# Retention and a two-layer ffn on one core: coefficients pinned behind retention, weights laid out by tiles, three raw buffers

## Chip, cores and metric

The kernel runs on one core of a Trainium2 chip. The time is device microseconds of one execution. Lower is better.

## What is computed

```python
def _attn_ref(q, k, v):                      # (4, 8, 576, 64) each
    scores = (1.0 / np.sqrt(D_)) * np.matmul(q, k.transpose(0, 1, 3, 2))
    gamma = 1.0 - 2.0 ** (-5.0 - np.arange(H, dtype=np.float32))
    Dmat = np.where(rel >= 0, gamma[:, None, None] ** rel[None, :, :], 0.0)
    return np.matmul(scores * Dmat[None, :, :, :], v)

def _moe_ref(x, w_in, w_out, a, b):          # x (2304, 512), w_in (512, 2048)
    h = x @ w_in
    P = a[0] + a[1] * h + a[2] * h**2 + a[3] * h**3
    Q = 1.0 + np.abs(b[0]) * np.abs(h) + np.abs(b[1]) * h**2
    return (P / (Q + 1e-06)) @ w_out

def _moe2_ref(x, w_in, w_out, s, b):
    r = np.maximum(x @ w_in, 0.0)
    return (s * (r * r) + b) @ w_out

# reference: x = _attn_ref(...) laid out (2304, 512); _moe_ref; then _moe2_ref
```

The weights `w_in` and `w_out` of both layers come as float64, everything else as float32. A float64 is read as two 32-bit words.

## The kernel before

**Retention** (`retention`, L147 to L293) runs over 16 pairs of heads. For each pair SP loads three tiles (`loads`, L173): `xT` (queries and keys, 576 KB), `vn` (values, 320 KB), `kn` (keys, 256 KB). They come from pools of `IN_BUFS` = 6 buffers; the load for a later pair waits until PE, and for `vn` POOL too, has done with the buffer. The loop over pairs (L276) issues, for pair p: the loads of pair p + 5; `value_state` (L237, PE: queries times the state left by earlier chunks); `state(p + 1)` (L225, PE, then ACT L228 and DVE L229); one step of cutting a weight; `scale(p + 3)` (L196, POOL multiplies values by a decay); `value_chunk` (L245, PE: masked scores times values; then DVE L248 makes `x`, ACT L250 its high part `xh`, POOL L251 its low part `xl`); `scores(p + 1)` (L214, PE; then DVE L217 multiplies by the mask into `pm`).

**Weights.** The ffn takes 32 weights kf: 16 column blocks in each of the two layers. One weight is 128 columns of `w_in` and the 128 rows of `w_out` that belong to them, 512 KB each. `w_load` (L100) brings both into a `raw` buffer with two DMAs on SP (L104, L106); there are `RAW_BUFS` = 2 such buffers. `w_cut` (L108) turns the words into a float32 number and splits it into a high and a low part, in five steps:

```python
pin(nc.scalar.activation(m, f, AF.Abs))                          # L120 ACT
pin(nc.vector.tensor_scalar(lo, lo, ...))                        # L121 DVE, end of step 1
pin(nc.vector.tensor_scalar(m, m, ...)); rest(...)               # L123, L124 DVE, step 2
rest(nc.vector.scalar_tensor_tensor(out=t, in0=hi, ...))         # L126 DVE, step 3
rest(nc.vector.scalar_tensor_tensor(out=hi..., in0=lo, ...))     # L129 DVE, step 4
rest(nc.scalar.copy(whf, f))                                     # L136 ACT, step 5
nc.gpsimd.tensor_tensor(out=wlf, in0=f, in1=f32(whf), ...)       # L137 POOL
next_load()                                                      # the next weight into a free raw buffer
```

The first three weights (`W_FIRST`) are cut within retention, one step in each turn of the pair loop from p = 1; the load of weight 2 is issued behind the low part of weight 0. The next weights are cut in the ffn.

**ffn** (L296). Blocks of 512 or 256 tokens times one weight make a unit u: 12 matmuls into `h` (L326 to L328), an activation on ACT, POOL and DVE (first layer L346 to L377, second L382 to L387), then 12 matmuls into `o` (L411), which DVE adds to `acc` (L423). `aneg` = -a (L513, DVE) and `babs` = |b| (L512, ACT) are its coefficients, from `a_sb` and `b_sb`, which `small_loads` (L253) loads.

**What sets the order.** Each engine, and SP's queue of loads, works through its own instructions strictly in order. The order comes from a scheduler that works with estimated times and may move an instruction forward if what it needs is there. `tc.keep_in_program_order` (`pin`, `dve`, `pe`) binds an instruction behind the one that was traced just before it on its engine, and only behind that one. Most of retention is pinned; `aneg`, `babs` and the small loads are not, nor are the cuts from weight 5 on (the first steps of weights 3 and 4 are).

Of the kernel before, what the change touches and what calls it, by code (L numbers as in the profile page):

```python
# [11 lines left out]
I32 = mybir.dt.int32  # L12
U32 = mybir.dt.uint32
I64 = mybir.dt.int64
AF = mybir.ActivationFunctionType
ALU = mybir.AluOpType
# [12 lines left out]
W_BUFS = 5  # L29
W_EARLY = 4  # L30
WTMP_BUFS = 1
RAW_BUFS = 2
IN_BUFS = 6
G_BUFS = 3
T_BUFS = {"ta": 2, "tq": 2, "tt": 4}
H_BUFS = 4
# [3 lines left out]


@with_exitstack
def retention_ffn_kernel(ctx, tc, w_in1, w_out1, a, b, w_in2, w_out2, s2, b2, qkv, maskv, gdec, out):
    nc = tc.nc
    B, H, S, D = SHAPE
    NT, DM = out.shape
    DFF = w_in1.shape[1]
    P = 128
    NP = H // 2
    NC = DM // P  # L50
    NF = DFF // P
    NCH = (S + P - 1) // P
    TAIL = S - (NCH - 1) * P
    NMAIN = S // P
# [23 lines left out]
        return t.bitcast(F32)  # L78


    w_src = [(w_in1, w_out1), (w_in2, w_out2)]
    w_raw = {}
    w_t = {}
    w_slots = {}
# [13 lines left out]
    w_slot_tiles(wpool, range(W_EARLY))  # L98

    def w_load(kf, eng, pin):  # L100
        layer, f = divmod(kf, NF)
        wi, wo = w_src[layer]
        w_raw[kf] = t = stg.tile([P, 2, DM], I64, tag="raw", name=f"raw{kf}")
        pin(eng.dma_start(out=t[:, 0, :].rearrange("p (c f) -> p c f", c=NC),  # L104
                          in_=wi[:, f * P:(f + 1) * P].rearrange("(c p) f -> p c f", p=P)))
        pin(eng.dma_start(out=t[:, 1, :], in_=wo[f * P:(f + 1) * P, :]))  # L106

    def w_cut(kf, pinned=False):  # L108

# [8 lines left out]
        pin(nc.scalar.activation(m, f, AF.Abs))  # L120
        pin(nc.vector.tensor_scalar(lo, lo, 2.0 ** 28, 2.0 ** 32 - 256, op0=ALU.add, op1=ALU.min))  # L121
        yield
        pin(nc.vector.tensor_scalar(m, m, 2.0 ** -15, None, op0=ALU.max))  # L123
        rest(nc.vector.tensor_scalar(t, t, 5, 2, op0=ALU.logical_shift_left, op1=ALU.logical_shift_right))  # L124
        yield
        rest(nc.vector.scalar_tensor_tensor(out=t, in0=hi, scalar=-0x40000000, in1=t,  # L126
                                            op0=ALU.bitwise_and, op1=ALU.bitwise_or))
        yield
        rest(nc.vector.scalar_tensor_tensor(out=hi.bitcast(U32), in0=lo, scalar=29, in1=t.bitcast(U32),  # L129
                                            op0=ALU.logical_shift_right, op1=ALU.bitwise_or))  # L130
        yield
        wh, wl = w_slots[kf % W_BUFS]
# [14 lines left out]
    def retention(actx):  # L147
# [25 lines left out]
        def loads(p, other=lambda: None):  # L173

            if p >= NPAIR:
                return
            n1, n2, n3 = 2 * S, 2 * S + NCH * P, 2 * S + NCH * P + NM
            xT[p] = sbr.tile([P, 2, S], F32, tag="xT", name=f"xT{p}")
            vn[p] = sbr.tile([P, NCH, 2, D], F32, tag="vn", name=f"vn{p}")
            kn[p] = sbr.tile([P, NMAIN, 2, D], F32, tag="kn", name=f"kn{p}")  # L180
            pin(nc.sync.dma_start(out=xT[p].rearrange("p x t -> p (x t)"), in_=qkv[p, :, 0:n1]))
            other()
            pin(nc.sync.dma_start(out=vn[p].rearrange("p c h d -> p (c h d)"), in_=qkv[p, :, n1:n2]))
            pin(nc.sync.dma_start(out=kn[p].rearrange("p c h d -> p (c h d)"), in_=qkv[p, :, n2:n3]))
# [75 lines left out]
        pin(nc.sync.dma_start(out=odec[:, :, 0:P], in_=gdec.rearrange("p (h t) -> p h t", t=P)))  # L260
        for p in range(1, IN_BUFS):
            loads(p)
            if p in (3, IN_BUFS - 1):
                next_load(nc.sync, pin)

        steps = (s for kf in range(W_FIRST) for s in w_cut(kf, True))
# [9 lines left out]
        for p in range(NPAIR):  # L276
            if p:
                loads(p - 1 + IN_BUFS)
            if p == 8:
                small_loads()  # L280
            value_state(p)
            if 0 < p < NPAIR - 1:
                state(p + 1)
            if p > 0:
                next(steps, None)
            scale(p + 3)
            value_chunk(p)
            if p + 1 < NPAIR:
                scores(p + 1)
            if p == 0:  # L290
                state(p + 1)
# [217 lines left out]
    nc.scalar.preload_act_table_set("natural_log_exp_and_others")  # L509
    with ExitStack() as actx:  # L510
        retention(actx)
    nc.scalar.activation(babs, b_sb, AF.Abs)  # L512
    nc.vector.tensor_scalar(aneg, a_sb, -1.0, None, op0=ALU.mult)  # L513
    with ExitStack() as fctx:
        ffn(fctx)


_INS = ["moe_w_in", "moe_w_out", "moe_a", "moe_b", "moe2_w_in", "moe2_w_out", "moe2_s", "moe2_b"]
_OUT = ((2304, 512), "float32")


# [56 lines left out]
```

## Time and profile before

| | us |
|---|---|
| runs (median of 3, lowest to highest) | 909.52 (907.26 to 909.61) |
| profiled execution | 911.61 |
| its span, first to last instruction | 909.8 |
| PE busy in the span | 872.0 (96%) |
| DVE, ACT, POOL busy | 603.4, 526.8, 358.4 |
| granted clock of TensorE, mean | 0.992 |

The span is the profiled execution's from its first to its last instruction; its own time also holds what lies around that. A share of busy time says little by itself: retention fills the first 95 us, the first layer runs to about 545 us, the second to the end, and each has another limit. The rows further below take them apart.

### The profile page before, as it was taken

To read this page: it belongs to the slowest core of one execution; us is meant where nothing else is said; L and a number is where in the kernel's file an instruction comes from. 1 tells how busy PE (TensorE), PEld (TensorE's weight loads), DVE (VectorE), ACT (ScalarE), POOL (GpSimd) and SP (SyncE) were. 2 spreads that over 40 slices of the span, in tenths; PEclk is the share of its full clock that TensorE was granted. 3 is DMA by queue.
4 is the path that set the end of the run, shared out by engine and by line. 5 is a ranking of instruction groups with operands and counts; after the bars stand their busy time and mean duration, and the time that the engine had idled before them with its cause. 6 is when DMAs were issued, how large, how long until landed. Compare 5 with 4: busy or idle time off the path is not lost.

```text
span 909.8 us, 12650 instructions
## 1 busy us (share of the span) xinstructions
PE 872.0 (96%) x4896; PEld 733.0 (81%) x4896; DVE 603.4 (66%) x905; ACT 526.8 (58%) x876; POOL 358.4 (39%) x248
## 2 busy tenths in 40 slices
PE   6798999999999999999999899999999999999997
PEld 6687787888788878878887678888888888888886
DVE  4587699697987887888998971435643465432334
ACT  2132688897877876777887574444444444443332
POOL 3486566576555565546688830111111111101000
PEclk9799999999999999999999999999999999999999
DMA  9972111111011111111101120111111012000013
GB/s 349 327 271 99 48 46 48 47 47 47 10 38 47 46 47 47 47 46 47 47 1 47 61 78 1 47 47 47 47 46 47 4 44 93 1 0 1 4 67 139
DMA packets 32317, 58.54 MB, mean 64 GB/s; under 512 B 2689, under 2 KB 19585, under 8 KB 32257
## 3 DMA queue, kind: packets, MB, share of 16 engines
q1 hardware_dynamic: 32256, 57.74, 18.2%
q8 instruction: 38, 0.62, 0.3%
q14 instruction: 23, 0.18, 0.1%
HBM read 53.01 MB, written 4.72 MB: 63 GB/s over the span
## 4 chain that ended last, share of the span: by engine, by line
PE 49%; DVE 21%; POOL 10%; DMA 9%; ACT 5%; issue 5%; SPq 1%; DVEq 0%; POOLq 0%; ACTq 0%
PE o L411 23%; PE h L328 8%; PE h L326 8%; PE h L327 8%; DMA raw<-in_moe_w_out_dram 6%; POOL wl L137 3%; DVE acc L423 2%; DVE tt L365 2%; POOL tq L348 2%; DVE h L366 2%; POOL gl L377 2%; DVE wm L126 2%; DVE tt L354 2%; DMA xT<-in_qkv_dram 2%; DVE raw L129 2%
## 5 line engine op out<-in xcount | busy, mean ns | idle before, releaser
L326 PE MATMUL h<-xl,wh 128*128 128x512 f32 (+1 forms) x640 | 236.6, 370 | 2.9 <-DVE tt L367 2.8
L327 PE MATMUL h<-xh,wl 128*128 128x512 f32 (+1 forms) x640 | 235.6, 368 | 0.0
L328 PE MATMUL h<-xh,wh 128*128 128x512 f32 (+1 forms) x640 | 235.5, 368 | 0.0
L137 POOL TENSOR_TENSOR wl<-raw,wh 128x1024 fp32r<-128x1024 f32 x32 | 80.0, 2501 | 278.2 <-ACT wh L136 278.2
L384 DVE TENSOR_SCALAR tt<-ta,s_sb,b_sb 128x512 f32<-128x512 f32 (+1 forms) x80 | 48.8, 610 | 143.1 <-ACT ta L383 142.9
L348 POOL TENSOR_TENSOR tq<-tq,ta 128x512 f32<-128x512 f32 (+1 forms) x80 | 104.1, 1301 | 100.2 <-ACT tq L347 98.3
L326 PEld LDWEIGHTS h<-xl,wh 128*128 128x128 f32 x640 | 120.5, 188 | 26.9 <-DVE tt L367 6.4
L328 PEld LDWEIGHTS h<-xh,wh 128*128 128x128 f32 x640 | 120.6, 188 | 20.4
L327 PEld LDWEIGHTS h<-xh,wl 128*128 128x128 f32 x640 | 120.6, 188 | 20.3
L411 PE MATMUL o<-gl,wh 128*128 128x512 f32 (+1 forms) x320 | 119.0, 374 | 8.8 <-POOL gl L377 6.2
L377 POOL TENSOR_TENSOR gl<-tt,gh 128x512 fp32r<-128x512 f32 (+1 forms) x80 | 105.0, 1314 | 34.0 <-ACT gh L372 31.7
L411 PE MATMUL o<-gh,wl 128*128 128x512 f32 (+1 forms) x320 | 117.9, 369 | 0.0
L411 PE MATMUL o<-gh,wh 128*128 128x512 f32 (+1 forms) x320 | 116.8, 368 | 0.0
L411 PE MATMUL o<-wh,gl 128*128 128x512 f32 x288 | 112.3, 390 | 0.4 <-DVE gl L387 0.4
L411 PE MATMUL o<-wh,gh 128*128 128x512 f32 x288 | 112.1, 389 | 0.0
L382 ACT ACTIVATE ta<-h 128x512 f32<-128x512 f32 (+1 forms) x80 | 44.3, 554 | 115.5 <-PE h L328 115.4
L411 PE MATMUL o<-wl,gh 128*128 128x512 f32 x288 | 94.0, 390 | 1.7 <-DVE acc L423 1.7
L386 ACT CAST gh<-tt 128x512 fp32r<-128x512 f32 (+1 forms) x80 | 46.2, 578 | 59.0 <-DVE tt L384 57.0
L387 DVE TENSOR_TENSOR gl<-tt,gh 128x512 fp32r<-128x512 f32 (+1 forms) x80 | 53.1, 664 | 39.4 <-ACT gh L386 39.4
L411 PEld LDWEIGHTS o<-gl,wh 128*128 128x128 f32 x320 | 60.2, 188 | 23.6 <-POOL gl L377 9.2
L423 DVE TENSOR_TENSOR acc<-acc,o 128x512 f32<-128x512 f32 (+1 forms) x114 | 69.5, 649 | 3.4 <-PE o L411 3.4
L359 ACT ACTIVATE ta<-tq,lnb 128x512 f32<-128x512 f32 (+1 forms) x80 | 54.6, 682 | 23.9 <-POOL tq L348 23.5
(51 smaller groups left out, 1414.7 us busy)
## 6 DMA issues: line engine op xcount, KB each, us to landing
raw<-in_moe_w_in_dram SPq DMA_DIRECT2D x32, 512.0 KB, 4.0
raw<-in_moe_w_out_dram SPq DMA_DIRECT2D x32, 512.0 KB, 4.9
xT<-in_qkv_dram SPq DMA_DIRECT2D x16, 576.0 KB, 7.2
vn<-in_qkv_dram SPq DMA_DIRECT2D x16, 320.0 KB, 6.6
out_dram<-acc SPq DMA_DIRECT2D x18, 256.0 KB, 2.2
kn<-in_qkv_dram SPq DMA_DIRECT2D x16, 256.0 KB, 6.9
mv<-in_maskv_dram SPq DMA_DIRECT2D x1, 310.0 KB, 4.2
odec<-in_gdec_dram SPq DMA_DIRECT2D x1, 256.0 KB, 5.7
```

Of the source, the lines that this page charges most:

```text
L137: nc.gpsimd.tensor_tensor(out=wlf, in0=f, in1=f32(whf), op=ALU.subtract)
L326: nc.tensor.matmul(ps, lhsT=wh[:, c, :], rhs=xl[:, c, r], start=c == 0, stop=False)
L327: nc.tensor.matmul(ps, lhsT=wl[:, c, :], rhs=xh[:, c, r], start=False, stop=False)
L328: nc.tensor.matmul(ps, lhsT=wh[:, c, :], rhs=xh[:, c, r], start=False, stop=c == NC - 1)
L348: nc.gpsimd.tensor_tensor(out=tq, in0=tq, in1=ta, op=ALU.mult)
L359: nc.scalar.activation(ta, tq, AF.Ln, bias=lnb, scale=QS)
L377: nc.gpsimd.tensor_tensor(out=gl, in0=tt, in1=f32(gh), op=ALU.subtract)
L384: nc.vector.tensor_scalar(tt, ta, s2_sb, b2_sb, op0=ALU.mult, op1=ALU.add)
L386: nc.scalar.copy(gh, tt)
L387: nc.vector.tensor_tensor(out=gl, in0=tt, in1=f32(gh), op=ALU.subtract)
L411: nc.tensor.matmul(ps, lhsT=lh, rhs=rh, start=st and x == 0, stop=sp and x == 2)
L423: nc.vector.tensor_tensor(out=at, in0=at, in1=ps, op=ALU.add)
```

## The change

1. `aneg` and `babs` are pinned behind what was traced before them: the last pair of retention.
2. The host lays the weights out by tiles: one array `w`, in which weight kf is 128 rows of 8 KB, `w_in` and `w_out` side by side. `w_load` issues one DMA of 1 MB in place of two.
3. `RAW_BUFS` goes from 2 to 3, `IN_BUFS` from 6 to 5. Weight 0 is loaded behind pair 2's inputs, weight 1 behind pair 4's, weight 2 in turn 2 behind pair 6's. The loop over pairs loads pair p + 4.
4. The steps of the first three cuts start in turn 3 and end in turn 14, which has two of them.

```diff
 W_BUFS = 5
 W_EARLY = 4
 WTMP_BUFS = 1
-RAW_BUFS = 2
-IN_BUFS = 6
+RAW_BUFS = 3
+IN_BUFS = 5
...
     def w_load(kf, eng, pin):
-        layer, f = divmod(kf, NF)
-        wi, wo = w_src[layer]
-        w_raw[kf] = t = stg.tile([P, 2, DM], I64, tag="raw", name=f"raw{kf}")
-        pin(eng.dma_start(out=t[:, 0, :].rearrange("p (c f) -> p c f", c=NC),
-                          in_=wi[:, f * P:(f + 1) * P].rearrange("(c p) f -> p c f", p=P)))
-        pin(eng.dma_start(out=t[:, 1, :], in_=wo[f * P:(f + 1) * P, :]))
+        w_raw[kf] = t = stg.tile([P, 2 * DM], I64, tag="raw", name=f"raw{kf}")
+        pin(eng.dma_start(out=t, in_=w[kf]))
...
         for p in range(1, IN_BUFS):
             loads(p)
-            if p in (3, IN_BUFS - 1):
+            if p in (2, 4):
                 next_load(nc.sync, pin)
...
             if p:
                 loads(p - 1 + IN_BUFS)
+            if p == 2:
+                next_load(nc.sync, pin)
...
-            if p > 0:
+            for _ in range((p > 2) + (p > 13)):
                 next(steps, None)
...
-    nc.scalar.activation(babs, b_sb, AF.Abs)
-    nc.vector.tensor_scalar(aneg, a_sb, -1.0, None, op0=ALU.mult)
+    tc.keep_in_program_order(nc.scalar.activation(babs, b_sb, AF.Abs))
+    tc.keep_in_program_order(nc.vector.tensor_scalar(aneg, a_sb, -1.0, None, op0=ALU.mult))
...
+def _by_tiles(w_in, w_out, P=128):
+    dm, dff = w_in.shape
+    wi = w_in.reshape(dm // P, P, dff // P, P).transpose(2, 1, 0, 3).reshape(dff // P, P, dm)
+    return np.ascontiguousarray(np.concatenate([wi, w_out.reshape(dff // P, P, dm)], axis=2)).view(np.int64)
```

How the order moves. The numbers behind the names are buffers and differ between the two kernels; a line of the changed kernel is lower by 4 to 6 (L121 is now L115, L513 now L509).

DVE of the kernel before, in turns 1 and 2: `x` of pair 1, then `aneg`, then the masked scores `pm` of pair 2 and the cut step 2 of weight 0.

```order
L229 TENSOR_TENSOR spre_108<-pv_252,spre_108 128x128
L121 TENSOR_SCALAR raw_136<-raw_136 128x1024
L248 TENSOR_TENSOR x_277<-pv_227,odec 128x576
L513 TENSOR_SCALAR aneg<-a_sb 128x4
L217 TENSOR_TENSOR pm_0_293<-sc_0_281,mv 128x576
L217 TENSOR_TENSOR pm_1_295<-sc_1_282,mv 128x576
L229 TENSOR_TENSOR spre_109<-pv_311,spre_109 128x128
```

`aneg` stands here in front of the masked scores of pair 2; in the changed kernel these come straight after `x` of pair 1, and the cut of weight 0 begins two turns later.

DVE of the changed kernel, from the last turns into the ffn (`raw_292` is weight 2, `raw_602` weight 3, `tt` the ffn's).

```order
L123 SCALAR_TENSOR_TENSOR raw_292<-raw_292,wm_843 128x1024
L242 TENSOR_TENSOR x_1013<-pv_937,odec 128x576
L211 TENSOR_TENSOR pm_0_1029<-sc_0_1017,mv 128x576
L211 TENSOR_TENSOR pm_1_1031<-sc_1_1018,mv 128x576
L242 TENSOR_TENSOR x_1051<-pv_987,odec 128x576
L509 TENSOR_SCALAR aneg<-a_sb 128x4
L115 TENSOR_SCALAR raw_602<-raw_602 128x1024
L350 TENSOR_TENSOR tt_1101<-tt_1101,h_1086 128x512
L351 SCALAR_TENSOR_TENSOR tt_1101<-tt_1101,aneg,h_1086 128x512
L350 TENSOR_TENSOR tt_1134<-tt_1134,h_1119 128x512
```

`aneg` and the first step of weight 3 (L115, in the kernel before it stood ahead of pair 11's `pm`) now stand between the last pair's `x` and the first operation of the ffn.

SP of the kernel before, behind pair 5's keys: weight 1, then the small loads around the inputs of pair 6.

```order
L181 DMA xT_145<-in_qkv_dram 128x1152
L183 DMA vn_146<-in_qkv_dram 128x640
L184 DMA kn_147<-in_qkv_dram 128x512
L104 DMA raw_151<-in_moe_w_in_dram 128x4x128
L106 DMA raw_151<-in_moe_w_out_dram 128x512
L254 DMA a_sb<-in_moe_a_dram 128x4
L181 DMA xT_238<-in_qkv_dram 128x1152
L255 DMA b_sb<-in_moe_b_dram 128x2
L256 DMA s_sb<-in_moe_s_dram 128x1
L257 DMA b_sb<-in_moe_b_dram 128x1
```

The first of the small loads is the one that `aneg` waits for; weight 1 stands behind pair 5's inputs.

SP of the changed kernel, from pair 4's values on (`raw_144` is weight 1).

```order
L177 DMA vn_139<-in_qkv_dram 128x640
L178 DMA kn_140<-in_qkv_dram 128x512
L100 DMA raw_144<-in_w_dram 128x1024
L248 DMA a_sb<-in_moe_a_dram 128x4
L249 DMA b_sb<-in_moe_b_dram 128x2
L250 DMA s_sb<-in_moe_s_dram 128x1
L251 DMA b_sb<-in_moe_b_dram 128x1
L175 DMA xT_230<-in_qkv_dram 128x1152
L177 DMA vn_231<-in_qkv_dram 128x640
L178 DMA kn_232<-in_qkv_dram 128x512
L175 DMA xT_286<-in_qkv_dram 128x1152
L177 DMA vn_287<-in_qkv_dram 128x640
```

Weight 1 and the four small loads now stand ahead of pair 5's inputs; weight 2 (`raw_292`) follows two rows further on, behind pair 6's.

DVE of the changed kernel in the ffn, where units 14 to 16 are worked on (`raw_1001` and `wm_1707` are weight 5, `wm_1941` weight 6).

```order
L363 SCALAR_TENSOR_TENSOR tt_1691<-h_1676,tt_1691 128x256
L115 TENSOR_SCALAR raw_1001<-raw_1001 128x1024
L350 TENSOR_TENSOR tt_1737<-tt_1737,h_1722 128x256
L351 SCALAR_TENSOR_TENSOR tt_1737<-tt_1737,aneg,h_1722 128x256
L361 SCALAR_TENSOR_TENSOR tt_1737<-tt_1737,aneg,h_1722 128x256
L362 SCALAR_TENSOR_TENSOR h_1722<-tq_1736,h_1722 128x256
L363 SCALAR_TENSOR_TENSOR tt_1737<-h_1722,tt_1737 128x256
L117 TENSOR_SCALAR wm_1707<-wm_1707 128x1024
L118 TENSOR_SCALAR wm_1707<-wm_1707 128x1024
L120 SCALAR_TENSOR_TENSOR wm_1707<-raw_1001,wm_1707 128x1024
L123 SCALAR_TENSOR_TENSOR raw_1001<-raw_1001,wm_1707 128x1024
L350 TENSOR_TENSOR tt_1782<-tt_1782,h_1767 128x512
```

Weight 5's steps stand here in one piece and weight 6's follow two rows later; before, they were spread over units 5 to 10. From about unit 25 on, DVE's cut operations stand at the same places as before, each for a weight one further on.

## Rows read from the trace of the kernel before

**Rows 1.** By stage: us; PE, PEld, DVE, ACT, POOL busy (instructions); clock; DMA share; GB/s
```profile
0.00:96.00 96.00, 76.73 (x1155) 70.92 (x1156) 59.98 (x87) 23.15 (x40) 52.81 (x38) 0.93 0.72 259
96.00:545.00 449.00, 435.27 (x2077) 361.11 (x2077) 386.37 (x576) 355.42 (x592) 278.82 (x199) 1.00 0.13 43
545.00:910.00 365.00, 359.96 (x1666) 300.92 (x1664) 157.07 (x243) 148.23 (x245) 26.74 (x11) 1.00 0.12 39
```

**Rows 2.** PE in time order: start, us, operation [idle before <-releaser]; turns 2, 3
```profile
21.77 0.99 PE L237 MATMUL pv<-xT,spre 64*64 64x128 f32 x16
30.33 2.85 PE L245 MATMUL pv<-pm,vn 128*64 128x128 f32 x20 [6.76 <-DVE pm L217]
35.44 1.43 PE L237 MATMUL pv<-xT,spre 64*64 64x128 f32 x16
```

**Rows 3.** DVE in time order, the work that PE waited for in turn 2
```profile
29.45 0.17 DVE L513 TENSOR_SCALAR aneg<-a_sb 128x4 f32<-128x4 f32 x1 [7.61 <-DMA a_sb<-in_moe_a_dram]
```

**Rows 4.** PE in time order, turns 11 and 12; then DVE within turn 11
```profile
70.86 0.99 PE L237 MATMUL pv<-xT,spre 64*64 64x128 f32 x16
75.89 0.43 PE L245 MATMUL pv<-pm,vn 128*64 128x128 f32 x2 [2.46 <-DVE pm L217]
80.27 1.21 PE L237 MATMUL pv<-xT,spre 64*64 64x128 f32 x16
...
73.55 1.62 DVE L121 TENSOR_SCALAR raw<-raw 128x1024 uint32<-128x1024 uint32 x1 [1.11 <-DMA raw<-in_moe_w_out_dram]
```

**Rows 5.** PE in time order, the last two turns and the first ffn matmul
```profile
88.56 0.99 PE L237 MATMUL pv<-xT,spre 64*64 64x128 f32 x16
92.55 0.99 PE L237 MATMUL pv<-xT,spre 64*64 64x128 f32 x16
95.26 0.50 PE L326 MATMUL h<-xl,wh 128*128 128x512 f32 x1
```

**Rows 6.** By stretch, columns as in rows 1: the clock and the DMA rate
```profile
10.00:15.00 5.00, 5.00 (x48) 4.76 (x50) 3.95 (x5) 0.39 (x1) 2.70 (x2) 1.00 1.03 406
30.00:35.00 5.00, 4.67 (x38) 4.18 (x40) 3.28 (x6) 1.03 (x3) 0.17 (x1) 0.50 0.94 312
35.00:40.00 5.00, 5.00 (x80) 4.68 (x80) 3.33 (x5) 0.27 (x1) 2.45 (x2) 0.86 0.95 335
```

**Rows 7.** DVE's two longest cut steps of weight 1; PE's turns 7 to 10
```profile
51.54 1.77 DVE L124 TENSOR_SCALAR wm<-wm 128x1024 int32<-128x1024 int32 x1
60.17 2.25 DVE L129 SCALAR_TENSOR_TENSOR raw<-raw,wm 128x1024 uint32<-128x1024 uint32 x1
...
51.93 0.99 PE L237 MATMUL pv<-xT,spre 64*64 64x128 f32 x16
57.76 0.99 PE L237 MATMUL pv<-xT,spre 64*64 64x128 f32 x16
61.75 0.99 PE L237 MATMUL pv<-xT,spre 64*64 64x128 f32 x16
66.87 0.99 PE L237 MATMUL pv<-xT,spre 64*64 64x128 f32 x16
```

**Rows 8.** POOL in time order, pair 5's values; SP's first load behind a cut
```profile
25.65 1.26 POOL L196 TENSOR_TENSOR vn<-vn,mv 128x640 f32<-128x640 f32 x1 [0.32 <-DMA vn<-in_qkv_dram]
...
49.76 0.38 SPq L104 DMA_DIRECT2D raw<-in_moe_w_in_dram  x1
```

**Rows 9.** ACT, then DVE, where the ffn begins
```profile
98.44 0.60 ACT L346 ACTIVATE ta<-h 128x512 f32<-128x512 f32 x1 [1.54 <-POOL xl L251]
...
99.80 0.69 DVE L354 TENSOR_TENSOR tt<-tt,h 128x512 f32<-128x512 f32 x1 [3.60 <-ACT tt L349]
```

**Rows 10.** Waits, whole program: total us, times, longest us
```profile
DVE raw L121 <- DMA raw<-in_moe_w_out_dram: 41.3, 22, 4.3
```

**Rows 11.** SP, then DVE: one load of the ffn and the step behind it
```profile
221.85 0.38 SPq L104 DMA_DIRECT2D raw<-in_moe_w_in_dram  x1
...
227.27 0.85 DVE L121 TENSOR_SCALAR raw<-raw 128x1024 uint32<-128x1024 uint32 x1 [4.22 <-DMA raw<-in_moe_w_out_dram]
```

More of the change, by code (lines that the diff above doesn't have):

```diff
@@ L42, in retention_ffn_kernel @@
 @with_exitstack
-def retention_ffn_kernel(ctx, tc, w_in1, w_out1, a, b, w_in2, w_out2, s2, b2, qkv, maskv, gdec, out):
+def retention_ffn_kernel(ctx, tc, a, b, s2, b2, w, qkv, maskv, gdec, out):
     nc = tc.nc
@@ L46, in retention_ffn_kernel @@
     NT, DM = out.shape
-    DFF = w_in1.shape[1]
     P = 128
@@ L50, in retention_ffn_kernel @@
     NC = DM // P
-    NF = DFF // P
+    NF = w.shape[0] // 2
     NCH = (S + P - 1) // P
@@ L78, in f32 @@
         return t.bitcast(F32)
-    w_src = [(w_in1, w_out1), (w_in2, w_out2)]
     w_raw = {}
@@ L100, in w_load @@
     def w_load(kf, eng, pin):
-        layer, f = divmod(kf, NF)
-        wi, wo = w_src[layer]
-        w_raw[kf] = t = stg.tile([P, 2, DM], I64, tag="raw", name=f"raw{kf}")
-        pin(eng.dma_start(out=t[:, 0, :].rearrange("p (c f) -> p c f", c=NC),
-                          in_=wi[:, f * P:(f + 1) * P].rearrange("(c p) f -> p c f", p=P)))
-        pin(eng.dma_start(out=t[:, 1, :], in_=wo[f * P:(f + 1) * P, :]))
+        w_raw[kf] = t = stg.tile([P, 2 * DM], I64, tag="raw", name=f"raw{kf}")
+        pin(eng.dma_start(out=t, in_=w[kf]))
     def w_cut(kf, pinned=False):
-        words = w_raw.pop(kf).rearrange("p w n -> p (w n)").bitcast(I32).rearrange("p (n two) -> p n two", two=2)
+        words = w_raw.pop(kf).bitcast(I32).rearrange("p (n two) -> p n two", two=2)
         lo, hi = words[:, :, 0].bitcast(U32), words[:, :, 1]
@@ L511, in retention_ffn_kernel @@
         retention(actx)
-    nc.scalar.activation(babs, b_sb, AF.Abs)
-    nc.vector.tensor_scalar(aneg, a_sb, -1.0, None, op0=ALU.mult)
+    tc.keep_in_program_order(nc.scalar.activation(babs, b_sb, AF.Abs))
+    tc.keep_in_program_order(nc.vector.tensor_scalar(aneg, a_sb, -1.0, None, op0=ALU.mult))
     with ExitStack() as fctx:
         ffn(fctx)
-_INS = ["moe_w_in", "moe_w_out", "moe_a", "moe_b", "moe2_w_in", "moe2_w_out", "moe2_s", "moe2_b"]
+_INS = ["moe_a", "moe_b", "moe2_s", "moe2_b"]
 _OUT = ((2304, 512), "float32")
@@ L564 @@
     given = {n: np.ascontiguousarray(inputs[n]) for n in _INS}
-    for n, arr in given.items():
-        if arr.dtype == np.float64:
-            given[n] = arr.view(np.int64)
+    given["w"] = np.concatenate([_by_tiles(np.asarray(inputs[n + "_w_in"]), np.asarray(inputs[n + "_w_out"]))
+                                 for n in ("moe", "moe2")])
     given["qkv"] = _by_pairs(*(np.asarray(inputs[n]) for n in "qkv"))
```

## The prediction

> **What bounds the kernel now.** I read the busy time by stage first. From 96 us on PE is the limit: it is busy for 435.27 of 449 us while the first layer runs and for 359.96 of 365 us in the second, at a granted clock of 1.00 [rows 1]. Before 96 us, in retention, it is not: 76.73 of 96 us at a clock of 0.93 [rows 1]. So a gain has to come mostly from retention, and I count there in turns of the pair loop. Turn k starts with the first matmul of L237 for pair k.
>
> A turn without trouble lasts 92.55 - 88.56 = 3.99 us, and the last one, which has no next pair, 95.26 - 92.55 = 2.71 us [rows 5]. Turn 2 starts at 21.77 [rows 2]. Thirteen such turns and the last would bring the first ffn matmul to 21.77 + 13 x 3.99 + 2.71 = 76.35 us. It starts at 95.26, so turns 2 to 15 hold 18.91 us of delay. Two turns have most of it. Turn 2 lasts 35.44 - 21.77 = 13.67 us: PE stands still for 6.76 us before the value matmuls [rows 2], because DVE stood for 7.61 us before `aneg`, an operation of 0.17 us that waits for the DMA of `a_sb` [rows 3]. The masked scores that PE needs are queued behind it. PE's clock is then at 0.50, its lower level of 1.2 GHz, from 30 to 35 us [rows 6], so the turn pays for the stall twice: 13.67 - 3.99 = 9.68 us. Turn 11 lasts 80.27 - 70.86 = 9.41 us: DVE's first cut step of weight 3 waits 1.11 us for its DMA and takes 1.62 us, and PE stands for 2.46 us behind it [rows 4]. That turn costs 5.42 us. The rest, 18.91 - 9.68 - 5.42 = 3.81 us, is cut steps that hold DVE up.
>
> **The change, part by part.**
> Coefficients behind retention. The pins put `aneg` on DVE and `babs` on ACT behind the last pair. The pin of weight 3's first steps binds them only to the instruction traced before them on their engine. That was `aneg` (or `babs`), which floated to the front and let them float too. With `aneg` held, weight 3's step goes behind the last pair as well, as the order shows. Both stalls leave: -9.68 and -5.42 us. Where the moved work goes, it is covered. DVE is idle for 3.60 us before its first ffn operation, ACT for 1.54 us [rows 9]; `aneg` (0.17) and the cut step (about 0.7 without contention, 1.62 at most) fit in the former, an Abs of a weight (about 1.2) and `babs` (0.2) just fit in the latter. I take 0. Without that cover it would be the 1.4 us on ACT.
>
> Cut steps two turns later. Each of the three first weights still costs DVE the same five steps, now in turns 3 to 14. In rows 7 a step costs PE's next turn what it exceeds the slack of DVE by: behind the step that ends with the 1.77 us operation (its first half took 1.15) turn 7 lasts 57.76 - 51.93 = 5.83 us, 1.84 too long, and behind the 2.25 us operation turn 9 lasts 66.87 - 61.75 = 5.12 us, 1.13 too long [rows 7]. Turn 8 between them lasts 3.99 [rows 7]. So a weight whose steps meet POOL's work costs 2.97 us, and one that does not costs about 0.1. Three weights are bounded by 0.3 and 8.9 us. Weight 0 came cheaply before because POOL stood still behind the stall; now nothing stands still, and POOL scales values until turn 12. I take two weights like weight 1 and one free one: 6.0 us. The whole delay of 18.91 us is thus exchanged for 6.0.
>
> Inputs and early weights on SP's queue. In the first pairs the DMA engines are full (share 1.03 at 406 GB/s, later 0.95 at 335) [rows 6], so a load lands when the bytes ahead of it have. Pair 5's values landed at 25.65 [rows 8], the last of 8246 KB by the sizes of the loads up to them. Now the second weight goes ahead of them: 1.05 MB, 2.6 us at 406 GB/s, so they land at 28.3 and are scaled (1.26 us [rows 8]) at 29.5. PE wants them behind the 0.99 us of matmuls with which turn 4 begins [rows 2], at 21.77 + 2 x 3.99 + 0.99 = 30.7. Pair 7's are the last of 12598 KB, 4.46 MB more: 11.0 us later at 406 GB/s, 13.3 at 335, so scaled at 37.9 to 40.2, and wanted in turn 6 at 38.7. The supply is just enough, with 0 to 1.5 us of delay. I take 0.6, since a fast DMA is the nearer row and the turns ahead run late by a cut step anyway. The four small loads stand ahead of pair 5 in SP's queue; they are only 4 KB, and nobody waits for them now. Five input buffers instead of six: pair k+5's load waits for pair k's last matmuls, and its values are wanted in turn k+4, three whole turns or 12 us later, against 1.18 MB or 3 us for its bytes. No cost. The load of weight 3 waits on SP for the low part of weight 0, as the load at 49.76 did [rows 8], now in turn 7, with pair 12's inputs behind it: about 49 us, landed by 57, wanted in turn 11 at about 62. No cost.
>
> Weights by tiles, three raw buffers. In the ffn one load of 1 MB takes the place of two halves. The two now land together 227.27 - 221.85 = 5.42 us after the first issue [rows 11], and DVE waits 41.3 us in 22 places for such loads [rows 10]. The third buffer would remove those waits if the cut of a weight stayed where it was and only its load came earlier. The order says otherwise: from the tenth weight on, DVE's cut operations stand in the same places as before, each for a weight one further on, so each first step again stands right behind its own load. I take the landing and so the waits as they were, 0 us. The bounds: the one issue saved, 0.38 us [rows 11], in 22 places is 8.4 us on DVE, and 41.3 us there go with only 449 - 435.27 = 13.73 us of idle PE [rows 1, 10], a third, so -3 us; a later landing is a rival below. The Trainium skill, "DMA: Bandwidth & Descriptors", section Bandwidth, speaks against the merged load: it lists 6.15 us for 1 MB (measured on another queue), which by an estimate would lengthen each wait by 0.7 us and bring the sum some 5 us closer to zero; no run here shows a single load of 1 MB yet.
> Weights 5 and 6 are now cut back to back between units 14 and 16 instead of being spread over units 5 to 10. The DVE work is the same, and units 5 to 10 are freed of it. If one weight's steps there found no cover, at contended lengths like 1.77 and 2.25 us [rows 7] for four of them, PE would stand for up to 7 us. I take 0, because DVE's order keeps the spread elsewhere, and 0 to +7 for the range.
>
> **The sum.** -18.91 + 6.0 + 0.6 + 0 = -12.3 us. The profiled execution has a span of 909.8 us and took 911.61; the median of the runs is 909.52, 2.1 below it. From the median: 909.5 - 12.3 = 897.2, say **897 us**. About 0.3%, 2.7 us, is what a measurement can tell from no change.
>
> **The rivals.**
> *The third buffer also pays in the ffn.* If the raw data are there when the first steps come, DVE's 41.3 us of waits go and with them up to all 13.7 us of idle PE: 897 - 13.7 = 883 at the end, 890 at half. For it: 22 waits. Against: the order. Chance 0.10.
> *The input supply becomes the bound.* One buffer fewer and three weights among the first seven pairs: if the DMA runs at 335 GB/s throughout and SP's hold at turn 7 delays pair 12, the turns lose 1.5 + 3 us, 3.9 more than I took: 901. The full DMA share speaks for it, the slack at pair 12 (landed by 57, wanted at 62) against. Chance 0.10.
> *The change doesn't clear the stalls*, because another early step waits instead: DVE's first step of weight 0 at turn 3 if its load were late. It lands before pair 3's inputs do, so I give 0.02; with 7 us of the 15 left, 904.
> *The merged load lands later: the slower side.* If one 1 MB transfer completes later than two overlapping halves, each first step on DVE holds the ffn chain longer. A third of the added wait reaches PE. The break-even is 12.3 x 3 / 22 = 1.7 us per load; if every wait became as long as the longest one, 4.3 us [rows 10], that adds 22 x (4.3 - 1.9) = 53 us on DVE and 17.6 on PE: 915, slower. A smaller lengthening gives 902. For it: waits ending exactly at a DMA. Against: the same bytes by the same engines. The figure of the Trainium skill's page on DMA, above, points this way. Chance 0.06, half of it slower than before or the same.
>
> **How the numbers follow.** The forecast has 0.72. Its own bounds (cut steps 0.3 to 8.9, supply 0 to 1.5, ffn -3 to +7) give 888 to 908 at their extremes; they hardly fall together. The range of 890 to 903.5 leaves out the second half of the first rival, the far end of the merged load, and unlikely sums: some 0.2. Faster by over 0.3% needs less than 906.8: 0.93. Within 0.3%: 0.04. Slower: 0.03.
>
> **What would show it.** Right: no wait of DVE for `a_sb` and no first step of weight 3 in retention; PE's clock at 1.00 from 20 us on; the first ffn matmul at about 83 us (76.35 + 6.6); turns of 4 us with three to five of 5 to 6 us; first steps in the ffn still waiting for DMA about 1.9 us each. Wrong: DVE or POOL waiting for `vn` in turns 4 to 7, a load that takes over 6 us to land, a stall of PE of several us around units 14 to 16, or first steps that no longer wait, with PE idle in the first layer well under 13 us.

## The result, and the profile after

| | before | changed kernel |
|---|---|---|
| runs, median (lowest to highest), us | 909.57 | 898.07 (897.12 to 899.73) |
| ratio to before, 95% interval | | 0.9881 (0.9859 to 0.9903) |
| profiled execution, its span, us | 911.61, 909.8 | 898.2, 896.4 |
| first ffn matmul | 95.26 | 84.60 |
| from there to the end of the span | 814.5 | 811.8 |
| granted clock, mean | 0.992 | 0.997 |

The change makes the kernel faster by 11.5 us of 909.57; 897 was forecast. Of the 13.4 us by which the spans differ, 10.66 lie before the first ffn matmul and 2.7 behind it. The profiled execution of the kernel before took 2.0 us more than its median and that of the changed kernel 0.1, so by the medians only some 0.8 us are left for the ffn (11.5 - 10.66).

By stage, columns as in [rows 1]; the stages are cut 11 to 12 us earlier than there:

```profile
0.00:84.00 84.00, 69.69 (x1144) 64.49 (x1146) 58.77 (x84) 21.90 (x38) 50.25 (x37) 1.00 0.78 296
84.00:534.00 450.00, 437.59 (x2102) 365.14 (x2097) 394.88 (x583) 358.96 (x595) 283.58 (x201) 1.00 0.13 45
534.00:896.00 362.00, 358.08 (x1658) 299.31 (x1656) 152.94 (x238) 147.93 (x243) 26.72 (x11) 1.00 0.11 37
```

The clock in retention is 1.00 where it was 0.93. The next rows are PE's in time order (start, us, operation, [idle before <- what ended it]): turn 4, the start of turn 5 (the view ends within that row), turn 13, and the first ffn matmul, which answers to the last of [rows 5].

```profile
32.91 0.89 PE L219 MATMUL pv<-vn,kn 128*64 128x128 f32 x16 [2.50 <-POOL vn L190]
...
35.98 0.76 PE L231 MATMUL pv<-xT,spre 64*64 64x128 f32 x10
...
74.11 0.89 PE L219 MATMUL pv<-vn,kn 128*64 128x128 f32 x16 [1.05 <-issue]
...
84.60 0.50 PE L322 MATMUL h<-xl,wh 128*128 128x512 f32 x1
```

Turn 2 lasts 3.99 us now, where it took 13.67 [rows 2], and nothing of weight 3 stands in turn 11. What is left is a new stall of 2.50 us in turn 4, released by POOL, and turns 5, 7, 9 and 13, which are 0.54 to 2.32 us too long behind cut steps. DVE in time order, turn 13 and the end of retention:

```profile
71.57 1.77 DVE L118 TENSOR_SCALAR wm<-wm 128x1024 int32<-128x1024 int32 x1
...
85.45 1.05 DVE L509 TENSOR_SCALAR aneg<-a_sb 128x4 f32<-128x4 f32 x1
86.42 0.68 DVE L115 TENSOR_SCALAR raw<-raw 128x1024 uint32<-128x1024 uint32 x1
```

`aneg` and weight 3's first step run behind the last pair with no wait before them, as the order had it (`aneg` takes 1.05 us there, not 0.17). In the ffn, the whole program's waits for the raw words (total us, times, longest), the landing of a weight (KB, median us from issue), and PE's longest stall:

```profile
DVE raw L115 <- DMA raw<-in_w_dram: 23.6, 18, 3.3
...
raw<-in_w_dram SPq DMA_DIRECT2D x32, 1024.0 KB, 4.8
...
170.50 0.47 PE L322 MATMUL h<-xl,wh 128*128 128x512 f32 x1 [3.95 <-DVE tt L363]
...
171.94 0.63 PE L324 MATMUL h<-xh,wh 128*128 128x512 f32 x1
```

DVE waits 23.6 us where it waited 41.3 [rows 10]; a load lands after 4.8 us where the pair of halves took 5.42 [rows 11]; over all 32 pairs the median is 5.3. The stall of 3.95 us is new. It is paid twice: the granted clock, 1.00 from 165 to 170 us, is 0.51 from 171.5 to 175 us, and eight matmuls from 171.51 us on take 3.4 us, where at the spacing before them (0.227 us) they would take 1.8.

### The profile page after: what moved, and what is told of

Same layout as the page of the kernel before. It is cut to its first block, busy times and chain, and to the rows that moved or that the text cites. A ratio compares the mean times of both kernels' runs of the same rounds, so it can differ in the third digit from the quotient of the medians.

```text
span 896.4 us, 12551 instructions
## 1 busy us (share of the span) xinstructions
PE 865.4 (97%) x4896; PEld 728.9 (81%) x4896; DVE 606.6 (68%) x905; ACT 528.8 (59%) x876; POOL 360.6 (40%) x248
## 4 chain that ended last, share of the span: by engine, by line
PE 47%; DVE 18%; POOL 6%; DMA 5%; ACT 4%; issue 2%; DVEq 0%; POOLq 0%; ACTq 0%
PE o L407 24%; PE h L322 8%; PE h L324 8%; PE h L323 8%; DMA raw<-in_w_dram 5%; POOL wl L131 3%; DVE acc L419 3%; DVE wm L120 2%; DVE raw L123 2%; DVE tt L350 2%; DVE tt L361 2%; POOL tq L344 1%; DVE h L362 1%; DVE wm L118 1%; DVE tt L363 1%
```

## The experiments

Each runs beside the kernel before on the same chip; ratios are to that. "ffn" is the time from the first ffn matmul to the end of the span. It and the first ffn matmul come from one execution, the profiled one, which lies within 1.1 us of the median in every kernel but the one before (2.0 over).

| kernel | median (range), us | ratio, 95% | first ffn matmul | ffn |
|---|---|---|---|---|
| before + the two pins | 896.76 (895.98 to 897.22) | 0.9864 (0.9848 to 0.9881) | 84.29 | 810.8 |
| before + tiles | 899.52 (899.02 to 899.76) | 0.9896 (0.9881 to 0.9910) | 91.73 | 805.5 |
| changed − pins | 903.59 (902.30 to 906.15) | 0.9945 (0.9925 to 0.9964) | 92.13 | 810.4 |
| before + pins + tiles | 892.56 (889.85 to 893.69) | 0.9821 (0.9799 to 0.9843) | 84.77 | 806.6 |
| changed, weight 5 unpinned | 891.89 (890.81 to 892.21) | 0.9816 (0.9798 to 0.9834) | 85.38 | 803.6 |
| changed, small loads in turn 8 | 896.93 (895.58 to 897.58) | 0.9866 (0.9851 to 0.9881) | 84.28 | 811.5 |
| changed, small loads on ACT | 898.30 (897.77 to 899.64) | 0.9899 (0.9881 to 0.9917) | 84.95 | 810.8 |
| before + pins + tiles, cuts in 15 turns | **887.30** (886.03 to 888.25) | 0.9766 (0.9747 to 0.9785) | 78.55 | 807.0 |
| cuts behind retention | 905.96 (one run) | | 84.67 | |
| all together | 888.19 (886.38 to 888.29) | 0.9772 (0.9757 to 0.9786) | 80.13 | 806.3 |
| all, small loads early | 889.76 (889.22 to 890.59) | 0.9795 (0.9782 to 0.9808) | 82.17 | 806.0 |

### Which part brings the gain: pins alone, tiles alone, all but the pins

```diff
-    nc.scalar.activation(babs, b_sb, AF.Abs)
-    nc.vector.tensor_scalar(aneg, a_sb, -1.0, None, op0=ALU.mult)
+    tc.keep_in_program_order(nc.scalar.activation(babs, b_sb, AF.Abs))
+    tc.keep_in_program_order(nc.vector.tensor_scalar(aneg, a_sb, -1.0, None, op0=ALU.mult))
```

> The kernel before with the two pins alone. My theory (the two stalls of retention are due to where aneg and the first step of weight 3 stand): DVE no longer waits for a_sb, turns 2 and 11 fall from 13.67 and 9.41 us to 4 to 6 us, the first ffn matmul comes at 80 to 84 us instead of 95.3, and the ffn takes as long as before (814.5 us from there to the end), so the time is 896 to 899 us, nearly all of the change's gain. Rival (the layout and the buffers carry a large part of the gain): 902 us or more.

The pins alone give 12.0 us, the whole of the gain. The first ffn matmul stands at 84.29, and turns 2 to 14 last 3.98 to 5.86 us:

```profile
84.29 0.50 PE L326 MATMUL h<-xl,wh 128*128 128x512 f32 x1
```

The ffn, expected at 814.5 us, takes 810.8. Apart from `aneg`, `babs` and the first step of weight 3, the order on every engine in the ffn is that of the kernel before, and up to 2.0 of these 3.7 us are what that kernel's profiled execution took beyond its median. Where the rest comes from was not tried.

The changed kernel with this edit taken back:

> The changed kernel with the two pins taken back. My theory: aneg stands on DVE ahead of pair 1's x and waits there for a_sb, which landed at 26.8 us in the changed kernel, so PE stands still in turn 1 for about 5 to 7 us and its clock falls; the first step of weight 3 stands within retention again but its load may have landed. The first ffn matmul at 91 to 96 us, the time 904 to 910 us. Rival (other parts of the change keep the stalls away): 898 to 900 us.

The stall returns, in turn 2 and not in turn 1 as I had expected, and with it 7.5 us of the first ffn matmul's gain (92.13). The time, 903.59 us, lies between the two ranges given, 0.4 us below that of the theory. PE, then DVE, in turn 2 of that kernel:

```profile
28.54 1.55 PE L219 MATMUL pv<-vn,kn 128*64 128x128 f32 x16 [6.62 <-issue]
...
27.61 0.17 DVE L509 TENSOR_SCALAR aneg<-a_sb 128x4 f32<-128x4 f32 x1 [8.17 <-DMA a_sb<-in_moe_a_dram]
```

The same `aneg`, of the same 0.17 us, waits 8.17 us for its DMA, and the matmul runs at the lower clock behind the stall (1.55 us for what takes 0.89).

Tiles alone, in the kernel before:

```diff
-        pin(eng.dma_start(out=t[:, 0, :].rearrange("p (c f) -> p c f", c=NC),
-                          in_=wi[:, f * P:(f + 1) * P].rearrange("(c p) f -> p c f", p=P)))
-        pin(eng.dma_start(out=t[:, 1, :], in_=wo[f * P:(f + 1) * P, :]))
+        pin(eng.dma_start(out=t, in_=w[kf]))
```

> The kernel before with the weights laid out by tiles alone, one load of 1 MB for each weight. My theory: both stalls of retention stay (first ffn matmul at 93 to 96 us); a load lands 4.8 us after its issue, against 5.4 us for the two halves, so DVE's waits for raw weights in the ffn fall from 41.3 us to 22 to 30 us, and the ffn takes 1 to 3 us less than 814.5: 906 to 909 us. Rival (the third buffer is what shortens the waits): they stay near 41 us and the time at 909 to 910 us.

This was missed by some 7 us: 899.52. The order on DVE, ACT and POOL is that of the kernel before to the last instruction, and on PE but for two matmuls of one group, so only the loads differ. PE and DVE in turn 2, the waits, and the landing:

```profile
30.33 2.85 PE L239 MATMUL pv<-pm,vn 128*64 128x128 f32 x20 [7.36 <-DVE pm L211]
...
29.44 0.17 DVE L507 TENSOR_SCALAR aneg<-a_sb 128x4 f32<-128x4 f32 x1 [7.62 <-DMA a_sb<-in_moe_a_dram]
...
DVE raw L115 <- DMA raw<-in_w_dram: 27.7, 19, 3.7
...
raw<-in_w_dram SPq DMA_DIRECT2D x32, 1024.0 KB, 4.8
```

The stall of turn 2 is untouched. Turn 11 shrinks (from 9.41 to 6.69 us), and the ffn by 9.0 us: each weight lands some 0.5 us sooner (4.8 against 5.3, the medians), 0.5 us x 22 waits is 11 us, and 13.6 us of DVE's waits go. Per microsecond of wait, 9.0 of 13.6 is far more than the third that I had reckoned. But the kernel before is read from an execution 2.0 us over its median: the medians differ by 9.3 us and the first ffn matmuls by 3.5, which leaves 5.8 for the ffn. The next pair is cleaner.

### What the third buffer does in the ffn

Before with pins and tiles, but two raw buffers, six of inputs and the early loads and steps where they were:

> The kernel before with the two pins and the weights by tiles, but with two raw buffers, six input buffers, and the cut steps and loads of the first weights where they were. My theory now (the gains of the pins, in retention, and of the merged load, in the ffn, add; the third buffer and the new order of the early weights give nothing and cost up to 4 us): first ffn matmul at 83 to 85 us as with the pins alone (84.3), the ffn takes 805 to 808 us as with the tiles alone (805.5), time 890 to 893 us, 5 to 8 us below the changed kernel. Rival (the ffn time of the run with the tiles alone came of where weight 3's first step stood, not of the tiles): the ffn takes 810 to 812 us, time 896 to 898 us.

Against the pins alone, whose order it has, the tiles take 4.2 us off the ffn (810.8 to 806.6) and 14.2 off DVE's waits (38.3 to 24.1): 0.30 of the wait, about the third. The time is 892.56 us, 5.5 below the changed kernel; the first ffn matmul is where it was (84.77 against 84.60), but the ffn is 806.6, not 811.8. So the rest of the change (a third buffer, one input buffer less, the cuts two turns later) makes the ffn 5.2 us longer. The bound of a pin moves with the buffers: first steps are pinned for weights below `W_FIRST + RAW_BUFS`, which was 5 and became 6. DVE of the changed kernel ahead of the stall at 170.50:

```profile
160.02 2.01 DVE L117 TENSOR_SCALAR wm<-wm 128x1024 f32<-128x1024 f32 x1 [0.90 <-ACT wm L114]
162.06 0.70 DVE L118 TENSOR_SCALAR wm<-wm 128x1024 int32<-128x1024 int32 x1
162.79 1.22 DVE L120 SCALAR_TENSOR_TENSOR wm<-raw,wm 128x1024 int32<-128x1024 int32 x1
...
164.53 2.11 DVE L123 SCALAR_TENSOR_TENSOR raw<-raw,wm 128x1024 uint32<-128x1024 uint32 x1
...
169.08 0.68 DVE L115 TENSOR_SCALAR raw<-raw 128x1024 uint32<-128x1024 uint32 x1
169.68 0.68 DVE L363 SCALAR_TENSOR_TENSOR tt<-h,tt 128x512 f32<-128x512 f32 x1
```

Weight 5's steps stand in one piece, weight 6's first step (169.08) follows, and `tt` (169.68), which PE waits for, is behind all of them. With the bound set back:

```diff
-        pin = tc.keep_in_program_order if kf < W_FIRST + RAW_BUFS else free
+        pin = tc.keep_in_program_order if kf < W_FIRST + 2 else free
```

> The changed kernel, with the pin on weight 5's first steps taken away (with three raw buffers the bound of the pinned weights had moved from 5 to 6). My theory (this pin holds weight 5's steps back until weights 5 and 6 are cut in one piece at units 14 to 16, and PE stands still for 3.95 us there): DVE's order is spread again, the stall of 3.95 us goes, the ffn takes 806 to 809 us instead of 811.8, time 893 to 896 us. Rival (the third buffer itself causes the crowd or another stall takes its place): ffn 811 us or more, time 897 to 899 us.

The ffn takes 803.6 us, 8.2 less, and the longest pause of PE there is:

```profile
172.29 0.50 PE L407 MATMUL o<-gl,wh 128*128 128x512 f32 x1 [0.80 <-POOL gl L373]
```

So the crowd was real. The gain is larger than I had expected (806 to 809), and only half of it lies where the crowd stood: when 1008 of the ffn's 3744 matmuls are done, some 210 us after the first, the two kernels are 4.2 us apart. Another 3.9 us come up to the 1584th, some 330 us after the first, in a stretch where the order on DVE and PE differs too; what makes them was not tried. Whether a third buffer is itself worth 3 us (803.6 against 806.6) or the order that came with it is, this pair doesn't tell; the last two runs come back to it.

### What holds up the turns: no cuts in them, smaller cuts in them

Two raw and six input buffers with the pins, tiles and no cut step inside the loop:

```diff
-            for _ in range((p > 2) + (p > 13)):
-                next(steps, None)
```

> The kernel with pins and tiles, no cut step within the pair loop; the three cuts run behind the last pair. My theory (cut steps are all that holds the turns up once the stalls are gone): every turn from 2 to 14 lasts 3.98 to 4.1 us and PE's last value matmul ends at 75 to 77 us, against about 84 with the cuts inside. The first ffn matmul then waits for weight 0, some 8 to 11 us, and weights 1 and 2 follow late, so the whole is slower than with the cuts inside: 893 to 905 us. Rival (the turns are long for another reason, such as the inputs): turns above 4.3 us remain.

PE at the last turn and at the first ffn matmul:

```profile
73.82 0.99 PE L231 MATMUL pv<-xT,spre 64*64 64x128 f32 x16
...
84.67 1.22 PE L318 MATMUL h<-xl,wh 128*128 128x512 f32 x2 [8.07 <-ACT wh L130]
```

Turns 2 to 14 all last 3.98 to 3.99 us: nothing but the cut steps, with the loads that follow a cut (and, in the changed kernel, the supply of turn 4), lengthens a turn. Their work is not free elsewhere: PE then waits 8.07 us for the first weight and later 8.54 us behind DVE's `tt` (at 108.12 us), and the kernel takes 905.96, 1 us more than the range that I had given.

The kernel with pins and tiles, where the second cut step, the longest, becomes two, and steps fill turns 1 to 15:

```diff
         pin(nc.vector.tensor_scalar(m, m, 2.0 ** -15, None, op0=ALU.max))
+        if pinned:
+            yield
         rest(nc.vector.tensor_scalar(t, t, 5, 2, op0=ALU.logical_shift_left, op1=ALU.logical_shift_right))
```

> The kernel with pins and tiles (two raw buffers, six input buffers), and step 2 of the three early cuts parted in two, so that no turn holds two of DVE's tensor_scalar operations; the three cuts then fill all turns from 1 to 15. My theory (a step costs the next turn what it exceeds DVE's slack of about 1.2 us by): the turns behind step 2, some 1.2 to 2.3 us too long each, fall to 0.6 us or less, the first ffn matmul comes 2 to 4 us earlier than with step 2 whole, at 80 to 82 us. Rival (the delay follows from POOL's operations being blocked, however the steps are cut): no earlier than 83.5 us.

887.30 us, with the first ffn matmul at 78.55 and turns of 3.98 to 4.95 us: the best of all these kernels, 5.3 us better than without the split. It starts earlier than the 80 to 82 us that I had expected. The same DVE work costs PE some 6 us less (84.77 to 78.55) when no turn holds much more of it than DVE's slack.

### Why pair 5's values come late in turn 4

SP's loads in the changed kernel (start, us of the issue) around weight 1, then by stretch (columns as in [rows 1]):

```profile
14.32 0.33 SPq L100 DMA_DIRECT2D raw<-in_w_dram  x1
16.81 0.33 SPq L248 DMA_DIRECT2D a_sb<-in_moe_a_dram  x1
18.24 0.33 SPq L249 DMA_DIRECT2D b_sb<-in_moe_b_dram  x1
20.61 0.33 SPq L250 DMA_DIRECT2D s_sb<-in_moe_s_dram  x1
21.29 0.33 SPq L251 DMA_DIRECT2D b_sb<-in_moe_b_dram  x1
22.77 0.33 SPq L175 DMA_DIRECT2D xT<-in_qkv_dram  x1
23.60 0.33 SPq L177 DMA_DIRECT2D vn<-in_qkv_dram  x1
```
```profile
22.00:24.00 2.00, 2.00 (x44) 1.93 (x42) 1.25 (x3) 0.27 (x1) 1.70 (x2) 1.00 0.94 350
24.00:25.00 1.00, 1.00 (x22) 0.93 (x18) 0.65 (x1) 0.00 (x0) 1.00 (x2) 1.00 0.39 81
25.00:26.00 1.00, 1.00 (x20) 0.93 (x20) 0.58 (x2) 0.67 (x1) 1.00 (x1) 1.00 0.60 110
```

The DMA engines, full until then, fall to 81 and 110 GB/s (379 and 358 in the kernel before): they had the end of weight 1 and the small loads to move, and pair 5's inputs, issued from 22.77 us on, bring the rate back to 379 only at 27 us. From the issue and landing time of each load I counted at most eight in flight; from 6.9 to 26.7 us, each issue comes within 0.1 us of the landing of the load eight before it. The four small loads move 4 KB, but each takes one of the eight places, for 6.6 to 10.0 us, and the 576 KB of `xT` behind them is issued at 22.77. Moved to turn 8, behind the inputs that matter:

```diff
-            nc.sync.dma_start(out=a_sb, in_=a.partition_broadcast(P))
+            pin(nc.sync.dma_start(out=a_sb, in_=a.partition_broadcast(P)))
```

(and so the other three).

> The changed kernel with the four small loads pinned where they are written, in turn 8, so that pair 5's inputs stand right behind weight 1 on SP. My theory (the small loads held pair 5's loads back, and the DMA fell to 81 to 110 GB/s from 24 to 26 us): that gap closes, pair 5's values land by 28.5 us instead of 31.6, PE's stall of 2.50 us in turn 4 goes, the first ffn matmul comes at 81.5 to 83 us instead of 84.6, the time is 895 to 897 us. Rival (the bytes of weight 1 ahead of pair 5 cause the stall): the stall stays at 2 us or more and the time at 897.5 to 899 us.

Pair 5's first load is then issued 5.8 us earlier:

```profile
17.00 0.33 SPq L175 DMA_DIRECT2D xT<-in_qkv_dram  x1
```

Its values land at 28.27 us, where they landed at 31.43 in the changed kernel, and the stall of turn 4 is gone, with the order on the other engines untouched. But of its 2.5 us only 0.3 are gained at the first ffn matmul (84.28). POOL, DVE and PE around turn 13 of that kernel:

```profile
67.41 2.40 POOL L131 TENSOR_TENSOR wl<-raw,wh 128x1024 fp32r<-128x1024 f32 x1
...
68.32 2.04 DVE L117 TENSOR_SCALAR wm<-wm 128x1024 f32<-128x1024 f32 x1
70.40 1.63 DVE L118 TENSOR_SCALAR wm<-wm 128x1024 int32<-128x1024 int32 x1
...
72.80 1.54 PE L219 MATMUL pv<-vn,kn 128*64 128x128 f32 x16 [1.92 <-issue]
```

The pairs are earlier against POOL's `wl`, so the cut step runs beside it (2.04 and 1.63 us, where 1.04 and 1.77 stood in the changed kernel), PE's pause is 1.92 us in place of 1.05, and the matmuls behind it run at the lower clock (1.54 for 0.89). Turn 13 takes 7.58 us: the stall has moved.

The same four loads, written in turn 1 so that they stand at about the same place in time, but from ACT:

```diff
-            nc.sync.dma_start(out=a_sb, in_=a.partition_broadcast(P))
+            pin(nc.scalar.dma_start(out=a_sb, in_=a.partition_broadcast(P)))
```

> The changed kernel with the same four small loads, issued at the same time (turn 1, about 17 us) from ACT's queue in place of SP's; nothing else moves on any engine. Theory A (they hold places in SP's queue, so the inputs behind them are issued too late): the DMA rate stays at 350 GB/s or more from 22 to 27 us, pair 5's first load is issued at about 17 us as in e4_small8 (22.8 in the changed kernel), and the stall of 2.50 us in turn 4 is gone. Theory B (their many tiny packets themselves take the DMA engines' time): the rate falls again to some 100 GB/s for about 2 us and a stall of 1.5 to 2.5 us stays in turn 4. Either way the total is within 1.5 us of the changed kernel's 898, since later cut steps take the place of the stall, as in e4_small8.

Neither theory as written. SP's last load of pair 5 and those behind it, ACT's first and last small load and the `spre` behind them, and PE at the start of turn 2:

```profile
19.57 0.33 SPq L178 DMA_DIRECT2D kn<-in_qkv_dram  x1
25.73 0.33 SPq L175 DMA_DIRECT2D xT<-in_qkv_dram  x1
27.31 0.33 SPq L177 DMA_DIRECT2D vn<-in_qkv_dram  x1
28.77 0.33 SPq L178 DMA_DIRECT2D kn<-in_qkv_dram  x1
29.61 0.45 SPq L100 DMA_DIRECT2D raw<-in_w_dram  x1
```
```profile
20.24 0.38 ACTq L248 DMA_DIRECT2D a_sb<-in_moe_a_dram  x1
...
23.16 0.34 ACTq L251 DMA_DIRECT2D b_sb<-in_moe_b_dram  x1
23.60 0.27 ACT L222 COPY spre<-pv 128x128 f32<-128x128 f32 x1 [7.21 <-DMA kn<-in_qkv_dram]
```
```profile
24.25 1.36 PE L231 MATMUL pv<-xT,spre 64*64 64x128 f32 x16 [3.21 <-DVE spre L223]
```

Pair 5 is issued from 16.65 us on and turn 4's stall is gone, as theory A says. But ACT got its four loads out only between 20.24 and 23.16 us, since they too waited for a place, and held up `spre` behind them by 7.21 us, which PE missed for 3.21 us before it could begin turn 2; SP meanwhile stood from 19.57 to 25.73, and the rate fell to 147 GB/s a little later (27 to 28 us). With both engines' loads counted together the sum is again eight at most. So the places are common to the two queues, and theory A was wrong to put them on SP's alone.

This run also shows what a place is. ACT's first small load had landed at 26.35 us, so that only seven loads were in flight, and yet SP issued at 27.31, 28.77 and 29.61 us, each within 0.1 us of the landing of the load eight before (pair 5's three, at 27.24, 28.75 and 29.59); at the last, only four others were in flight. In no run here is a load issued before the one eight before it, counted over both queues, has landed. It isn't the number in flight that is kept at eight: each load waits for one load, and a small load counts like a large one.

### All together, with the third buffer

The changed kernel with the bound of the pins, the split step in turns 1 to 15 and the small loads in turn 8; then the same with the small loads left early:

> The changed kernel (three raw buffers, five of inputs) with all that the earlier runs showed to pay: weight 5's first steps unpinned, the second cut step split into two turns (steps fill turns 1 to 15), the small loads issued in turn 8. Theory: turn 4's supply stall is gone, the first ffn matmul is at 78 to 80.5 us, the ffn lasts 803 to 807 us, in all 883 to 887 us; under 886 would mean that the third buffer is worth something beside the two-buffer version of the same schedule (887.3). Rival: the third buffer pays nothing once the landing is earlier and the cuts are spread: ffn at or over 806.5 us and 887 us or more.

> The kernel of e9_all with the small loads left to the scheduler, so that they stand ahead of pair 5's inputs on SP's queue. Theory: with DVE no longer behind, the supply stall of turn 4 (about 2.5 us before the value matmuls of pair 4, behind POOL's scaling of pair 5's values) delays all later turns: first ffn matmul 1.5 to 2.5 us later than in e9_all, the ffn of the same length. Rival: the cut steps take the place of the stall as they did where the small loads alone were moved: less than 0.5 us apart.

The second theory held: PE in turn 4 of the kernel with early small loads,

```profile
33.51 0.89 PE L221 MATMUL pv<-vn,kn 128*64 128x128 f32 x16 [3.16 <-POOL vn L192]
```

and its first ffn matmul is 2.04 us later, its total 1.6: where no cut step takes the stall's place, most of it is paid. The first theory fell: 888.19 us, with an ffn of 806.3, against 887.30 and 807.0 with two raw buffers. Its rival held but for 0.2 us of ffn (806.5 or more). With two buffers the ffn differs by 0.7 us and the total by 0.9 the other way, so in the sum three raw buffers are worth nothing here. Within the ffn two things cancel: by the 1008th matmul the kernel with three is 2.9 us behind the one with two, and by the 1584th it is 0.6 us ahead. It wins 3.5 us in the stretch in which the unpinned kernel above won 3.9 against its partner with two buffers, and it had lost the 2.9 before. Since the order on PE and DVE differs there as well, the buffer and the order are not told apart. The first ffn matmul is 1.6 us later, since PE waits for POOL's `vn` in turns 12 and 13 (pair 13's values land only at 63.0 us, behind the small loads; pair 14's stand on POOL behind a `wl`):

```profile
64.48 0.89 PE L221 MATMUL pv<-vn,kn 128*64 128x128 f32 x16 [0.48 <-POOL vn L192]
...
69.89 0.89 PE L221 MATMUL pv<-vn,kn 128*64 128x128 f32 x16 [1.35 <-POOL vn L192]
```

## Why the prediction was right

The sum was -12.3 us; the medians differ by 11.5 and the spans by 13.4. The mechanism that carries the gain, the two stalls and the pins that end them, was right. Of the smaller terms one was made up otherwise than forecast, one was mis-sized, and two errors in the ffn cancelled. By its steps:

- **Coefficients behind retention, right.** Both stalls left together, at the price of 0: `aneg` and weight 3's first step ran without a wait. The pins alone give 12.0 us. That weight 3 went along because its pin hung on `aneg` stands on the order and on this run.
- **Cut steps, 6.0, right in the sum.** From 21.44 (turn 2) a free run would end at 76.02 us; 84.60 is 8.58 later. Turns 5, 7, 9, 11 and 13 are too long by 1.23 + 0.54 + 2.32 + 0.10 + 1.73 = 5.9 us, and the kernel without steps in the loop has none of it. The make-up was not as forecast, so that the sum came out has luck in it: weights 0, 1 and 2 cost 1.8, 2.4 and 1.7 us, where two of 2.97 and one of about 0.1 had been taken.
- **Supply, 0.6 with bounds 0 to 1.5, mis-sized and misplaced.** It measured 2.58 us, in turn 4 and not turn 6. The step that failed is "they are only 4 KB, and nobody waits for them now". Nobody waits for them, but the loads behind them do: the loads were counted in bytes, and each waits for the load eight before it, however small. The bytes themselves were reckoned well: pair 5's values, forecast for 28.3 us, land at 28.27 with the small loads out of the way and at 31.43 with them. The cover that the prediction named ("the turns ahead run late by a cut step") worked the other way round: without the stall the later cut steps cost some 2 us more, and so it cost the total at most some 1 us in this kernel (898.07 against 896.93, with ranges that touch). The rival of the input supply (901 us) had the mechanism, though not its cause, and only part of its price.
- **ffn, 0 with bounds -3 to +7, right in its sum and wrong in its two terms; that they cancelled was luck.** It measured -2.7 by the spans, some -0.8 by the medians. "I take the landing and so the waits as they were" failed: the single load lands some 0.5 us sooner, and DVE's waits fell from 41.3 to 23.6 us. The third of a wait that reaches PE held with the pins in place (4.2 of 14.2 us); the pair without them gives more, 5.8 to 9.0 of 13.6. The Trainium skill, "DMA: Bandwidth & Descriptors", section Bandwidth, lists 6.15 us for 1 MB on another queue; the runs show 4.8 here, so the rival built beside it fell. The crowd of weights 5 and 6, taken at 0 since "DVE's order keeps the spread elsewhere", stands for 3.95 us of stall and some 1.6 of lower clock, inside the 0 to +7 of the range. The ladder of runs, each with the ffn's length: before 814.5; pins 810.8; and tiles 806.6; and the rest of the change 811.8; weight 5 unpinned 803.6. So -3.7 - 4.2 + 5.2 = -2.7. Of the first term, up to 2.0 us are the profiled execution before; the rest of it was not tried apart. The ladder is one way up: without the pins the tiles' step is larger, and taking the pins back from the changed kernel makes its ffn 1.4 us shorter (810.4), not longer.
- **The rival "the third buffer also pays"** had the right place for a gain in the ffn, but the runs give it to the landing: with pins and tiles DVE's waits are 24.1 us with two buffers, and 23.6 in the changed kernel with three. What the kernels with three buffers and weight 5 unpinned win later in the ffn (3.5 to 3.9 us) may be the buffer's or the order's.

## What to carry to other kernels

An instruction that waits for a DMA stops everything queued behind it on its engine, so pin the small, late-needed ones behind the work that must not wait; two such lines gave the whole 12 us. Then cut what remains into pieces that fit the slack of a turn: splitting one step gave 5 us more. Count loads and not only bytes: here each load waited for the eighth before it, and one of 1 KB counted like one of 1 MB. A bound that is written with a buffer count (`W_FIRST + RAW_BUFS`) moves when the count is changed.

## What the runs showed of the hardware

- At most eight loads were in flight, from SP and ACT together, and in no run was a load issued before the one eight before it had landed, even with only four others in flight (the small loads on ACT, 29.61 us). A load of 0.5 to 2 KB took 5.6 to 11.1 us from issue to landing in the crowd. Whether the chip or the program's semaphores set the eight was not tried.
- One load of 1 MB with 8 KB per partition lands after 4.8 us (median of 32); two of 512 KB issued behind each other, one of them in rows of 1 KB, after 5.3 (median of 32 pairs in the kernel before). Whether the size or the rows do it was not tried apart.
- A cut step that took 0.68 us on DVE with POOL idle took 2.04 beside POOL's work:

```profile
31.05 0.68 DVE L117 TENSOR_SCALAR wm<-wm 128x1024 f32<-128x1024 f32 x1
```

  is turn 2 of the kernel with tiles alone, behind its stall; the 2.04 us, beside `wl`, are those of the kernel with the small loads in turn 8, above.
